# Mixture of experts: the second product of experts 1 to 7 with features on partitions, written at a register's column

## The chip, the cores and the metric

The kernel runs on one core of a Trainium2 chip. A core has TensorE (PE, with its weight loads PEld), VectorE (DVE), ScalarE (ACT), GpSimd (POOL) and SyncE (SP), each with an instruction queue of its own that is worked off in order, and 16 DMA engines. The metric is the device time of one execution in microseconds; three runs of the kernel before took 546.01, 545.29 and 543.28 us, median 545.29.

## What is computed

Three parts, one after the other. (1) A decayed linear attention over 2 x 8 heads gives x, 1536 tokens of 512 features. (2) A mixture of 8 experts with top-1 routing. (3) A dense layer, 512 to 2048 to 512 features, with a rational function between its products. The change lies in (2) and at its border to (3):

```python
gate_w = probs[np.arange(N), expert_idx]
for i in range(N):                       # first come, up to `capacity` a expert
    e = expert_idx[i]
    if counts[e] < capacity:
        disp[e, counts[e]] = x[i]; pos[i] = counts[e]; counts[e] += 1; keep[i] = True
h = np.maximum(np.einsum('ecd,edf->ecf', disp, w1), 0.0)      # 512 -> 1024
y = np.einsum('ecf,efd->ecd', h, w2)                          # 1024 -> 512
out[i] = gate_w[i] * y[expert_idx[i], pos[i]]                 # for kept i
```

The gate is a positive number for each token, and relu(g x) = g relu(x) for such a number, so the gate may be put on x or on y.

## The kernel before, in words

Every float product is done as three TensorE products of float32r parts: a value is split into a high part (ACT copies it, `whi`, `xh`, `hh`, `yh`) and the rest (DVE subtracts, `wlo`, `xl`, `hl`, `yl`), and high x high, high x low and low x high are summed in PSUM.

*Experts.* The program is written out by hand in the order in which each engine gets it. An expert has 224 slots, gathered from memory by token number as two tiles of rows (128 and 96; `gather`, POOL) and turned by PE so that features lie on partitions (`expert_x`: four 128x128 transposes, L822, then ACT writes `xh`, L825, and DVE `xl`, L826). Expert 0 goes through a special path (`first_expert`), experts 1 to 7 through the loop in `moe`. First product: four steps `fp`, each 24 matmuls (L852 to L854) with 128x128 weights standing and 224 columns of x moving; ACT takes the relu of a step (L857), DVE its rest (L858). In steps 2 and 3 the x rows of the next expert are turned. Second product: 48 matmuls (L885 to L887) with a slice of h standing (128 or 96 slots) and 512 weight columns moving, in four quarters of 12; so y comes out with slots on partitions. `y_out` scales it by the gate (ACT, L730), and POOL scatters the rows to memory tensor `yd` (L799), sorted by expert.

*Back again.* In experts 6 and 7 and in the first steps of the dense layer the 12 tiles of 128 sorted rows are loaded (`y_load`, SP, L959, tile `yr`) and turned by PE (`y_tile`, L972, PSUM tile `ytp`) into `yh` and `yl`, which the dense layer reads with features on partitions.

*Beside it.* In each of the eight slots of an expert `prep_next` asks SP for a half weight tile (512 KB into `raw`, six buffers) and splits the next one (ACT L136, DVE L142). `dec_slot` decodes the dense layer's weights, which come as 64 bit numbers, at every third slot from the third step of expert 1: two ACT scalings of the loaded tile (L186, L187) into `gq`, in the next slot two DVE bit operations (L194, L195) and a POOL addition (L198) into `dw`, later a store by SP to `wd` (L222). Tiles `gq` and the load's have two buffers each, and so has `dw`. Weights and decode loads and stores are all in SP's one queue.

*Overflow.* If an expert has more rows than slots, a branch at the end of expert 1 (`overflow`, L907 loads the flag into a register of every engine, L908 branches) redoes all experts in loops. With these inputs the branch is not taken.

Of the kernel before, what the change touches and what calls it, by code (L numbers as in the profile page):

```python
# [1 line left out]

# [28 lines left out]
W = 128 + W2  # L31
GROUPS = (0, 4, 7, 10, 12)
# [43 lines left out]
class Build:  # L76
# [15 lines left out]
    def setup(self):  # L92
# [25 lines left out]
        self.ovi = c.tile([1, 1], I32, name="ovi")  # L118
        self.xd = tc.dram_tile([NT, DM], F32, name="xd")
# [354 lines left out]
    def counts(self):  # L474
        nc = self.nc
        nc.vector.tensor_copy(self.off, self.cnt)
        nc.vector.tensor_tensor(out=self.off[:, 0:1], in0=self.off[:, 0:1], in1=self.pad, op=ALU.add)
        nc.vector.tensor_reduce(out=self.ovf, in_=self.off[0:1, 0:E], axis=AX.X, op=ALU.max)
        nc.vector.tensor_scalar(
            out=self.ovi, in0=self.ovf, scalar1=float(min(W, self.cap)), scalar2=None, op0=ALU.is_gt  # L480
        )
# [7 lines left out]
    def rows(self):  # L489
# [13 lines left out]
            op=ALU.add,  # L503
        )
# [219 lines left out]
    def win_out(self, acc, j):  # L724
        self.y_out(acc, 0, j)

    def y_out(self, acc, e, j):
        r = (128, W2)[j]
        y = self.mp.tile([128, 512], F32, tag="y", name="y", bufs=3)
        self.nc.scalar.activation(out=y[0:r], in_=acc[0:r], func=AF.Copy, scale=self.gate(e, j)[0:r])  # L730
        self.scatter(y[0:r], e, j)

    def first_expert(self):
# [8 lines left out]
        self.win_out(acc, 0)  # L742
# [22 lines left out]
        self.win_out(acc, 1)  # L765
# [28 lines left out]
    def scatter(self, t, e, j):  # L794
        s = self.slot(e, j)
        self.apart("yd", self.put_rows(t, self.sidx[0 : t.shape[0], s : s + 1]))

# [10 lines left out]
    def apart(self, key, i):  # L808
# [3 lines left out]
        self.puts[key].append(i)  # L812

# [16 lines left out]
    def moe(self):  # L830
        nc = self.nc
        with ExitStack() as st:
            self.dp = self.pool("dec", stack=st)
# [7 lines left out]
            for e in range(1, E):  # L841
                xh, xl = (t.pop(e)[:, :, 0:W] for t in (self.xh, self.xl))
                hh, hl = {}, {}
                for fp in range(4):
# [16 lines left out]
                    self.prep_next()  # L861
                    if fp >= 2 and e + 1 < E:
# [3 lines left out]
                    if e == E - 2 and fp >= 2:  # L866
                        for m in range(2):
                            self.y_load(2 * (fp - 2) + m)
# [6 lines left out]
                for hf in range(2):  # L875
                    i = 4 * e + 2 + hf
                    wh, wl = self.whi[i], self.wlo[i]
                    for m in range(2):
                        r = (128, W2)[m]
                        ms = slice(m * 128, m * 128 + r)  # L880
                        for fl in range(4):
                            f = hf * 4 + fl
                            fh, fo = hh[f // 2][:, f % 2, ms], hl[f // 2][:, f % 2, ms]
                            ws = slice(fl * 512, fl * 512 + 512)
# [3 lines left out]
                        if (e, hf, m) == (1, 1, 1):  # L888
                            self.overflow()
                        self.prep_next()  # L890
                        if e == E - 2:
                            self.y_tile(2 * hf + m, self.bank("tp", "ytp"))
                            self.y_load(4 + 2 * hf + m)
                        if 1 <= e < 5 and 2 * hf + m < 3:
                            self.perm_put(3 * (e - 1) + 2 * hf + m)
                        if e == 5 and hf == 1 and m == 1:
                            self.perm_get()
                        if hf == 1:
                            self.y_out(acc[m], e, m)
                        self.dec_slot(8 * e + 4 + 2 * hf + m)  # L900
                        if e == E - 1:
                            self.ffn_step(2 * hf + m)
                    del self.whi[i], self.wlo[i]

    def overflow(self):
        nc, tc = self.nc, self.tc
        v = nc.values_load(self.ovi[0:1, 0:1], min_val=0, max_val=1, skip_runtime_bounds_check_because="a flag")  # L907
        with tc.If(v > 0):  # L908
# [53 lines left out]
    def y_tile(self, t, tp):  # L962
# [8 lines left out]
        for k in range(4):  # L971
            nc.tensor.transpose(tp[:, k], y[:, k * 128 : k * 128 + 128], self.col("ident"))  # L972
# [310 lines left out]
```

## Time and profile before

| | before |
|---|---|
| median of 3 runs | 545.29 us (543.28 to 546.01) |
| the profiled execution | 545.39 us, of which the span of instructions is 543.6 |
| mean granted TensorE clock | 0.989 of full |
| PE, PEld, DVE, ACT, POOL busy | 96%, 81%, 76%, 72%, 52% |
| moved by DMA | 89.55 MB, 165 GB/s over the span |

Parts by the trace's time: attention and routing to about 84 us, expert 0 to 104, experts 1 to 7 to about 290 (the dense layer's first four steps are woven into expert 7), the dense layer to the end. The span is the time from the first to the last instruction. Busy shares count instructions that compute; a group's "waits" are the idle time of an engine just before an instruction, put down to what ended last.

### The profile page before, as it was taken

The numbers are of one execution on the slowest core, as the hardware profiler recorded it, in microseconds if no ns is written. First come the engines' busy times: TensorE is split into PE (matmuls) and PEld (weight loads), VectorE is DVE, ScalarE is ACT, GpSimd is POOL, SyncE is SP. The second block draws the span as 40 slices with busy tenths as digits, with TensorE's granted clock in tenths as the row PEclk, the third lists the DMA queues.
The fourth block names the chain that finished last, engine by engine and source line by source line (L and its number), as shares of the span: only waits on it lengthen the run. The fifth ranks groups of instructions, "written<-read, shape, count | busy, mean of one in ns | idle before, by whom it ended". The sixth has DMA issues, their size and how long they took to land.

```text
span 543.6 us, 9843 instructions
## 1 busy us (share of the span) xinstructions
PE 524.5 (96%) x3674; PEld 440.5 (81%) x3674; DVE 415.0 (76%) x630; ACT 391.4 (72%) x634; POOL 282.3 (52%) x212
## 2 busy tenths in 40 slices
PE   9999899999999999979999999999999999999993
PEld 4888777888898898959888888888888888888883
DVE  3548975768758797857667798999899998865972
ACT  2788952776567675836579798999999988676750
POOL 5554314307565675303144445675757765535664
PEclk9999999999999999979999999999999999999998
DMA  8998735695999999995505001230222200000203
GB/s 290 395 335 324 245 110 165 182 332 174 315 273 402 279 363 295 368 356 181 193 31 194 0 1 39 62 121 14 77 77 79 78 1 0 1 0 2 78 21 136
DMA packets 31044, 89.55 MB, mean 165 GB/s; under 512 B 6222, under 2 KB 6478, under 8 KB 30992
## 3 DMA queue, kind: packets, MB, share of 16 engines
q1 hardware_dynamic: 27216, 78.38, 42.7%
q0 software_dynamic: 3776, 10.50, 5.4%
q8 instruction: 30, 0.49, 0.4%
q14 instruction: 22, 0.18, 0.1%
HBM read 75.22 MB, written 14.16 MB: 164 GB/s over the span
## 4 chain that ended last, share of the span: by engine, by line
PE 53%; DMA 13%; issue 4%; DVE 2%; ACT 2%; POOL 1%; POOLq 0%; SPq 0%; ACTq 0%
DMA raw<-wm 9%; PE h L994 8%; PE h L992 8%; PE h L993 8%; PE o L1065 7%; PE o L1063 7%; PE o L1064 7%; DMA r<-wf 2%; DMA yr<-yd 1%; PE l L885 1%; PE l L886 1%; PE l L887 1%; PE ytp L972 1%; PE l L852 1%; ACT whi L136 1%
## 5 line engine op out<-in xcount | busy, mean ns | idle before, releaser
L142 DVE TENSOR_TENSOR wlo<-raw,whi 128x1024 fp32r<-128x1024 f32 x80 | 112.7, 1415 | 25.9 <-ACT whi L136 25.1
L1043 POOL TENSOR_TENSOR gg<-fx,gg 128x512 fp32r<-128x512 f32 x47 | 61.1, 1299 | 69.4 <-issue 60.6
L136 ACT ACTIVATE whi<-raw 128x1024 fp32r<-128x1024 f32 x80 | 84.2, 1056 | 16.3 <-DMA raw<-wm 15.9
L1063 PE MATMUL o<-whi,gg 128*128 128x512 f32 x192 | 74.9, 390 | 0.0
L992 PE MATMUL h<-yh,whi 128*128 128x512 f32 x192 | 74.8, 390 | 0.0
L994 PE MATMUL h<-yh,wlo 128*128 128x512 f32 x192 | 74.7, 389 | 0.0
L1065 PE MATMUL o<-whi,gg 128*128 128x512 f32 x192 | 74.7, 389 | 0.0
L1064 PE MATMUL o<-wlo,gg 128*128 128x512 f32 x192 | 74.7, 389 | 0.0
L993 PE MATMUL h<-yl,whi 128*128 128x512 f32 x192 | 74.7, 389 | 0.0
L1018 POOL TENSOR_TENSOR fw<-fh,fw 128x512 f32<-128x512 f32 x48 | 64.4, 1341 | 11.0 <-ACT fw L1007 11.0
L1005 ACT ACTIVATE fx<-h,ab 128x512 f32<-128x512 f32 x48 | 37.4, 779 | 38.4 <-PE h L994 38.2
L852 PE MATMUL l<-xh,whi 128*128 128x224 f32 x224 | 62.2, 278 | 0.3 <-PEq L908 0.3
L854 PE MATMUL l<-xh,wlo 128*128 128x224 f32 x224 | 61.5, 275 | 0.0
L853 PE MATMUL l<-xl,whi 128*128 128x224 f32 x224 | 61.4, 274 | 0.0
L198 POOL TENSOR_TENSOR dw<-gq 128x512 int32<-128x512 int32 x16 | 24.9, 1558 | 56.0 <-DVE gq L195 32.5
L885 PE MATMUL l<-whi,hh 128*128 128x512 f32 (+1 forms) x112 | 45.7, 408 | 0.0
L887 PE MATMUL l<-whi,hl 128*128 128x512 f32 (+1 forms) x112 | 44.8, 400 | 0.0
L886 PE MATMUL l<-wlo,hh 128*128 128x512 f32 (+1 forms) x112 | 44.7, 399 | 0.0
L852 PEld LDWEIGHTS l<-xh,whi 128*128 128x128 f32 x224 | 43.0, 192 | 1.1 <-issue 0.7
L853 PEld LDWEIGHTS l<-xl,whi 128*128 128x128 f32 x224 | 43.0, 192 | 0.2
L1029 DVE SCALAR_TENSOR_TENSOR fw<-fw,cq,h 128x512 f32<-128x512 f32 x48 | 35.6, 742 | 9.8 <-ACT h L1024 9.8
L854 PEld LDWEIGHTS l<-xh,wlo 128*128 128x128 f32 x224 | 43.0, 192 | 0.0
(161 smaller groups left out, 1267.9 us busy)
## 6 DMA issues: line engine op xcount, KB each, us to landing
raw<-wm SPq DMA_DIRECT2D x64, 512.0 KB, 9.7
r<-wf SPq DMA_DIRECT2D x32, 512.0 KB, 6.6
vq<-vq SPq DMA_DIRECT2D x11, 512.0 KB, 6.0
kk<-kk SPq DMA_DIRECT2D x11, 512.0 KB, 6.4
wd<-dw SPq DMA_DIRECT2D x16, 256.0 KB, 9.7
raw<-wd SPq DMA_DIRECT2D x8, 512.0 KB, 6.5
xd<-xs SPq DMA_DIRECT2D x12, 256.0 KB, 4.5
yr<-yd SPq DMA_DIRECT2D x12, 256.0 KB, 2.9
```

Source lines behind the costliest of these rows:

```text
L136: nc.scalar.activation(out=self.whi[i][:, sl], in_=raw, func=AF.Copy)
L142: nc.vector.tensor_tensor(out=self.wlo[i][:, sl], in0=raw, in1=self.whi[i][:, sl].bitcast(F32), op=ALU.subtract)
L852: nc.tensor.matmul(ps[:, fi], lhsT=wh[:, sl], rhs=xh[:, k], start=(k == 0), stop=False)
L853: nc.tensor.matmul(ps[:, fi], lhsT=wh[:, sl], rhs=xl[:, k], start=False, stop=False)
L854: nc.tensor.matmul(ps[:, fi], lhsT=wl[:, sl], rhs=xh[:, k], start=False, stop=(k == 3))
L992: nc.tensor.matmul(h, lhsT=wh[:, sl], rhs=yh[:, k], start=(k == 0), stop=False)
L993: nc.tensor.matmul(h, lhsT=wh[:, sl], rhs=yl[:, k], start=False, stop=False)
L994: nc.tensor.matmul(h, lhsT=wl[:, sl], rhs=yh[:, k], start=False, stop=(k == 3))
L1018: nc.gpsimd.tensor_tensor(out=w, in0=h2, in1=w, op=ALU.mult)
L1063: self.nc.tensor.matmul(ps, lhsT=gh[:, ms], rhs=wh[:, ws], start=first, stop=False)
L1064: self.nc.tensor.matmul(ps, lhsT=gh[:, ms], rhs=wl[:, ws], start=False, stop=False)
L1065: self.nc.tensor.matmul(ps, lhsT=gl[:, ms], rhs=wh[:, ws], start=False, stop=last)
```

## The change

In experts 1 to 7 the second product is turned round: 128x128 slices of the weights stand, and the 224 slots of h move, so y comes out with features on partitions. It is 96 matmuls an expert, into two PSUM tiles of two 224-column parts. ACT and DVE write it straight into `yh` and `yl`, now one tile each of 1536 + 224 columns, at the column where the expert's tokens start; that number is read into a register of ACT and of DVE (`start`). What an expert writes past its own tokens is written over by the next. The gate goes onto the gathered x rows, in place, on ACT (`x_gate`). Expert 0 keeps its form; its two y tiles are scaled as before and turned by PE (`y_turn`). Gone are the scatter of y to memory (but in the overflow body), the loads of it and their transposes. The decode adds in place into the first half of `gq` and has no tile of its own. The overflow body takes its tiles from the buffers of hh and hl.

```diff
@@ class Build
     def dec_spill(self, n):
-        w = self.dp.tile([128, 512], I32, tag="dw", name="dw", bufs=2)
-        self.dec_dve(n, w)
-        self.w32[n] = w.bitcast(F32)
+        g = self.gq[n][0][:, 0]
+        self.dec_dve(n, g)
+        self.w32[n] = g.bitcast(F32)
...
-    def win_out(self, acc, j):
-        self.y_out(acc, 0, j)
-
-    def y_out(self, acc, e, j):
+    def y_rows(self, acc, j):
         r = (128, W2)[j]
-        y = self.mp.tile([128, 512], F32, tag="y", name="y", bufs=3)
-        self.nc.scalar.activation(out=y[0:r], in_=acc[0:r], func=AF.Copy, scale=self.gate(e, j)[0:r])
-        self.scatter(y[0:r], e, j)
+        y = self.wp.tile([128, 2, 512], F32, tag="wt", name="y", bufs=3)[0:r, 0]
+        self.nc.scalar.activation(out=y, in_=acc[0:r], func=AF.Copy, scale=self.gate(0, j)[0:r])
+        return y
+
+    def y_turn(self, y, j):
+        r = y.shape[0]
+        tp = self.bank("tp", "ytp").rearrange("p (k n) -> p k n", k=4)[:, :, 0:r]
+        for k in range(4):
+            self.nc.tensor.transpose(tp[:, k], y[:, k * 128 : k * 128 + 128], self.col("ident")[0:r, 0:r])
+        self.y_put(tp, slice(0, 4), bass.ds(self.start(0), r) if j else slice(0, r))
+
+    def y_put(self, ps, k, at):
+        yh, yl = self.yh[:, k, at], self.yl[:, k, at]
+        self.nc.scalar.activation(out=yh, in_=ps, func=AF.Copy)
+        self.nc.vector.tensor_tensor(out=yl, in0=ps, in1=yh.bitcast(F32), op=ALU.subtract)
+
+    def start(self, e):
+        lo, hi = (max(0, NT - (E - e) * W), NT) if e else (0, 128)
+        return self.nc.values_load(
+            self.st8[0:1, e : e + 1],
+            engines=(mybir.EngineType.Activation, mybir.EngineType.DVE),
...
@@ def first_expert(self):
-        self.win_out(acc, 0)
+        y = self.y_rows(acc, 0)
...
         self.win_l1(x, ps, 12, 18)
+        self.y_turn(y, 0)
         ht0 = self.win_split(h, 0, bank("l1"))
         self.win_l1(x, ps, 18, 24)
         self.win_relu(ps, h, 1)
+        self.x_gate(1, 0)
+        self.x_gate(1, 1)
         self.expert_x(1, 0)
...
-        self.win_out(acc, 1)
+        self.y0 = self.y_rows(acc, 1)
...
+    def x_gate(self, e, j):
+        x = self.xg[2 * e + j]
+        self.nc.scalar.activation(out=x, in_=x, func=AF.Copy, scale=self.gate(e, j))
...
@@ def moe(self):
                     self.prep_next()
+                    if 1 <= fp < 3 and e + 1 < E:
+                        self.x_gate(e + 1, fp - 1)
                     if fp >= 2 and e + 1 < E:
                         self.expert_x(e + 1, fp - 2)
...
                     self.dec_slot(8 * e + fp)
-                    if e == E - 1:
-                        self.y_tile(4 + fp, self.bank("tp", "ytp"))
-                        if fp >= 2:
-                            self.y_load(6 + fp)
-                acc = [self.bank("l2") for _ in range(2)]
...
-                            nc.tensor.matmul(acc[m][0:r], lhsT=fh, rhs=wh[:, ws], start=(f == 0), stop=False)
-                            nc.tensor.matmul(acc[m][0:r], lhsT=fh, rhs=wl[:, ws], start=False, stop=False)
-                            nc.tensor.matmul(acc[m][0:r], lhsT=fo, rhs=wh[:, ws], start=False, stop=(f == 7))
...
+                    if (e, fp) == (1, 0):
+                        self.y_turn(self.y0, 1)
+                acc = [self.bank("l2").rearrange("p (a n) -> p a n", a=2)[:, :, 0:W] for _ in range(2)]
+                for q in range(4):
+                    wh, wl = self.whi[4 * e + 2 + q // 2], self.wlo[4 * e + 2 + q // 2]
+                    for f in range(2 * q, 2 * q + 2):
+                        fh, fo = hh[f // 2][:, f % 2], hl[f // 2][:, f % 2]
+                        for o in range(4):
+                            ws = slice(f % 4 * 512 + o * 128, f % 4 * 512 + o * 128 + 128)
+                            mm = partial(nc.tensor.matmul, acc[o // 2][:, o % 2], skip_group_check=True)
+                            mm(lhsT=wh[:, ws], rhs=fh, start=(f == 0 and o % 2 == 0), stop=False)
+                            mm(lhsT=wh[:, ws], rhs=fo, start=False, stop=False)
+                            mm(lhsT=wl[:, ws], rhs=fh, start=False, stop=(f == 7 and o % 2 == 1))
+                    if (e, q) == (1, 3):
+                        self.overflow()
+                    self.prep_next()
...
+                    if q == 3:
+                        at = bass.ds(self.start(e), W)
+                        for i in range(2):
+                            self.y_put(acc[i], slice(2 * i, 2 * i + 2), at)
+                    self.dec_slot(8 * e + 4 + q)
+                    if e == E - 1:
+                        self.ffn_step(q)
...
@@ def build(arrays, capacity):
-    nc = bacc.Bacc("TRN2", target_bir_lowering=False, num_devices=1)
+    nc = bacc.Bacc("TRN2", target_bir_lowering=False, num_devices=1, dynamic_dma_scratch_size=8192)
```

## Rows read from the trace of the kernel before

**Rows 1.** The page, part 1: busy us, share of the span, instructions.
```profile
PE 524.5 (96%) x3674; PEld 440.5 (81%) x3674; DVE 415.0 (76%) x630; ACT 391.4 (72%) x634; POOL 282.3 (52%) x212
```
**Rows 2.** Waits of PE: what, for whom, us in total, times, longest.
```profile
PE ytp L972 <- DMA yr<-yd: 3.9, 1, 3.9
```
**Rows 3.** Windows: length, busy PE, PEld, DVE, ACT, POOL, clock, DMA share, GB/s.
```profile
150.00:172.00 22.00, 22.00 (x149) 19.39 (x149) 15.33 (x18) 14.42 (x22) 12.01 (x9) 1.00 0.98 320
...
231.00:236.00 5.00, 1.07 (x6) 0.64 (x5) 3.34 (x3) 0.49 (x1) 0.66 (x1) 0.87 1.03 397
236.00:242.00 6.00, 6.00 (x20) 4.22 (x18) 1.92 (x2) 2.67 (x4) 0.00 (x0) 0.54 1.02 398
```
**Rows 4.** Timeline of ACT, experts 2 and 3: start, us, operation, idle before.
```profile
141.66 0.66 ACT L186 ACTIVATE gq<-r 128x512 f32<-128x512 f32 x1 [1.56 <-DMA r<-wf]
...
150.30 0.69 ACT L186 ACTIVATE gq<-r 128x512 f32<-128x512 f32 x1
...
155.89 1.06 ACT L136 ACTIVATE whi<-raw 128x1024 fp32r<-128x1024 f32 x1 [0.30 <-DMA raw<-wm]
161.36 0.66 ACT L186 ACTIVATE gq<-r 128x512 f32<-128x512 f32 x1 [4.41 <-DMA r<-wf]
```
**Rows 5.** Timeline of PE around the first y tile, expert 6.
```profile
231.41 0.39 PE L887 MATMUL l<-whi,hl 128*128 128x512 f32 x1
235.73 1.09 PE L972 MATMUL ytp<-ct,yr 128*128 128x128 f32 x4 [3.93 <-DMA yr<-yd]
...
241.67 0.60 PE L972 MATMUL ytp<-ct,yr 128*128 128x128 f32 x4
```
**Rows 6.** Groups of PE by form: count, busy us, mean ns, idle before.
```profile
L972 PE MATMUL ytp<-ct,yr 128*128 128x128 f32 x48 | 7.4, 285 | 3.9 <-DMA yr<-yd 3.9
```
**Rows 7.** Timeline of PE, expert 3: the two turns of x rows.
```profile
157.53 0.60 PE L822 MATMUL tp<-ct,xg 128*128 128x128 f32 x4
...
160.65 0.60 PE L822 MATMUL tp<-ct,xg 128*128 128x128 f32 x4
```
**Rows 8.** Timeline of PE, experts 4 and 5: second product, then first.
```profile
189.20 0.39 PE L885 MATMUL l<-whi,hh 128*128 128x512 f32 x1
...
194.70 0.26 PE L852 MATMUL l<-xh,whi 128*128 128x224 f32 x1
...
202.74 0.60 PE L822 MATMUL tp<-ct,xg 128*128 128x128 f32 x4
```
**Rows 9.** Timeline of PE, expert 0: the turn of expert 1's first x rows.
```profile
96.99 0.60 PE L822 MATMUL tp<-ct,xg 128*128 128x128 f32 x4
```
**Rows 10.** Timeline of ACT in the same stretch.
```profile
97.18 0.59 ACT L697 ACTIVATE h<-l 96x512 f32<-96x512 f32 x1 [0.89 <-PE l L688]
97.68 0.58 ACT L825 ACTIVATE xh<-tp 128x512 fp32r<-128x512 f32 x1
```
**Rows 11.** Timeline of SP: issues of the stores of decodes 1, 2 and 3.
```profile
135.54 0.38 SPq L222 DMA_DIRECT2D wd<-dw  x1
...
139.32 0.53 SPq L222 DMA_DIRECT2D wd<-dw  x1
...
148.73 0.33 SPq L222 DMA_DIRECT2D wd<-dw  x1
```
**Rows 12.** Line 222 in the windows of these three issues: time to landing.
```profile
DMA to landing us min/median/max: 9.6/9.6/9.6
...
DMA to landing us min/median/max: 13.3/13.3/13.3
...
DMA to landing us min/median/max: 15.6/15.6/15.6
```
**Rows 13.** Line 907: ACT's load of the flag, ns.
```profile
L907 ACTq TENSOR_LOAD <-ovi x1: 460/460/460, 123.8 to 123.8; - x1
```
**Rows 14.** Waits of SP: its branch.
```profile
SPq L908 <- SPq L908: 7.6, 1, 7.6
```

More of the change, by code (lines that the diff above doesn't have):

```diff
@@ L1 @@
 from contextlib import ExitStack
+from functools import partial
 import concourse.bass as bass
@@ L503, in rows @@
             op=ALU.add,
+        )
+        nc.vector.scalar_tensor_tensor(
+            out=self.st8, in0=self.ov.to_broadcast([1, E]), scalar=float(NT), in1=off[0:1], op0=ALU.mult, op1=ALU.max
+        )
+        nc.vector.tensor_scalar(
+            out=self.st8[:, 0:1], in0=self.pad[0:1], scalar1=-1.0, scalar2=128.0, op0=ALU.mult, op1=ALU.add
         )
@@ L722, in win_l2 @@
             )
-    def win_out(self, acc, j):
-        self.y_out(acc, 0, j)
-    def y_out(self, acc, e, j):
+    def y_rows(self, acc, j):
         r = (128, W2)[j]
-        y = self.mp.tile([128, 512], F32, tag="y", name="y", bufs=3)
-        self.nc.scalar.activation(out=y[0:r], in_=acc[0:r], func=AF.Copy, scale=self.gate(e, j)[0:r])
-        self.scatter(y[0:r], e, j)
+        y = self.wp.tile([128, 2, 512], F32, tag="wt", name="y", bufs=3)[0:r, 0]
[16 more added lines that the diff above has]
+            engines=(mybir.EngineType.Activation, mybir.EngineType.DVE),
+            min_val=lo,
+            max_val=hi,
+            skip_runtime_bounds_check_because="no expert before it exceeds its slots, or all go behind the last row",
+        )
     def first_expert(self):
@@ L927, in overflow @@
                 for fh in range(2):
-                    w = self.yp.tile([128, 4, 512], F32, tag="yl1", name="ow", bufs=1)
-                    nc.sync.dma_start(out=w.rearrange("p k n -> p (k n)"), in_=wm[fh])
+                    w = [tmp(f"hl{k}") for k in range(4)]
+                    for k in range(4):
+                        nc.sync.dma_start(out=w[k], in_=wm[fh][:, k * 512 : k * 512 + 512])
                     for f in range(4 * fh, 4 * fh + 4):
@@ L940, in overflow @@
                             )
[L941 removed]
+                        nc.scalar.activation(out=hs[fh][:, fs], in_=ps, func=AF.Relu)
                 py = self.bank("l1", "opy")
                 for fh in range(2):
[L944 to L945 removed]
+                    w = [tmp(f"hl{k}") for k in range(4)]
+                    for k in range(4):
+                        nc.sync.dma_start(out=w[k], in_=wm[2 + fh][:, k * 512 : k * 512 + 512])
                     for f in range(4 * fh, 4 * fh + 4):
@@ L955, in overflow @@
                 self.put_rows(xg, gi[:, 1:2])
-    def y_load(self, t):
-        y = self.xp.tile([128, DM], F32, tag="xg", name="yr", bufs=4)
-        self.nc.sync.dma_start(out=y, in_=self.yd[t * 128 : t * 128 + 128, :])
-        self.yr[t] = y
-    def y_tile(self, t, tp):
-        nc = self.nc
-        tb, r = divmod(t, 4)
-        if r == 0:
-            p = self.yp if tb < 2 else self.fp
-            self.yh[tb] = p.tile([128, 4, 512], F32R, name=f"yh{tb}")
-            self.yl[tb] = p.tile([128, 4, 512], F32R, name=f"yl{tb}")
-        y = self.yr.pop(t)
-        tp = tp.rearrange("p (k n) -> p k n", k=4)
-        for k in range(4):
-            nc.tensor.transpose(tp[:, k], y[:, k * 128 : k * 128 + 128], self.col("ident"))
-        sl = slice(r * 128, r * 128 + 128)
-        nc.scalar.activation(out=self.yh[tb][:, :, sl], in_=tp, func=AF.Copy)
-        nc.vector.tensor_tensor(
-            out=self.yl[tb][:, :, sl], in0=tp, in1=self.yh[tb][:, :, sl].bitcast(F32), op=ALU.subtract
-        )
+            with tc.For_i(0, NTILE, 1) as t:
+                y = tmp("hh0")
+                rows = self.yd.rearrange("(t p) n -> t p n", p=128)[bass.ds(t, 1)]
+                nc.sync.dma_start(out=y, in_=rows.rearrange("one p n -> (one p) n"))
+                tp = self.bank("tp", "otp").rearrange("p (k n) -> p k n", k=4)
+                for k in range(4):
+                    nc.tensor.transpose(tp[:, k], y[:, k * 128 : k * 128 + 128], self.col("ident"))
+                self.y_put(tp, slice(0, 4), bass.ds(t * 128, 128))
     def ffn_at(self, n):
@@ L1106, in ffn @@
             self.fp = self.pool("ffn", stack=st)
-            for t in range(10, NTILE):
-                self.y_load(t)
             for n in range(4, NA):
@@ L1130, in ffn_step @@
         self.ffn_do("g")
-        for t in {4: (8, 9), 5: (10, 11)}.get(n, ()):
-            self.y_tile(t, self.bank("tp" if n == 4 else "l2", "ytp"))
         if not soon:
@@ L1144, in ffn_step @@
             self.ffn_p(n - 1)
-        self.ffn_b([(n - lb, m) for m in range(2 if n == lb else 4)])
+        self.ffn_b([(n - lb, m) for m in range(4)])
         self.put_outs()
```

78 lines of the change are left out of this document (26 added, 52 removed).

## The prediction

> **What bounds the kernel now.** I read the page's engine row first: PE is busy for 96% of the span and beside its own weight loads (81%) nothing passes 76% [rows 1]. Then the waits of PE: one item stands out, the transposes of the y rows that come back from memory, 3.9 us in one wait [rows 2]. The windows say what the clock did there: 0.87 granted in the stretch with the wait, 0.54 in the 6 us behind it, and 1.00 in the expert stretch shown [rows 3]; 2.4 GHz is full, 1.2 GHz half. So before the wait PE runs without a hole; what shortens the time is fewer TensorE microseconds, or that hole. The DMA column has a second reading: share 0.98 in expert 3 and 1.02 to 1.03 around the hole. The transfers are the resource that is nearly full, and ACT (ScalarE), in order, waits for them: 4.41 us before one gq decode [rows 4]. PE does not feel that today, since only relu results, split x and weights come to it from ACT, and the last relu of an expert is first read three quarters into an 11 us product.
>
> The sum is made against the profiled execution's 545.39 us (span 543.6), which is 0.1 us from the median of the three runs, 545.29.
>
> **What is removed.**
> 1. *The hole.* The last matmul before it starts at 231.41 and would be followed 0.23 later; the transposes start at 235.73: 4.1 us. From 235.73 to 241.67, 5.94 us, PE does one tile's transposes and 12 matmuls at half clock [rows 5]. At full clock that is 0.44 + 12 x 0.229 = 3.19 (both worked out below), so 2.75 more. The yr<-yd load that ended the wait no longer exists. Together 6.85.
> 2. *Transposes.* 48 of them in 12 tiles [rows 6]. In expert 3 two tiles' starts, 157.53 and 160.65, are 3.12 apart with 24 matmuls of 0.1117 between (2.68), so four transposes with the restart cost 0.44 [rows 7]. 12 x 0.44 = 5.3.
> 3. *Second product.* Before: 24 matmuls of 512 columns from 189.20 to 194.70, 0.229 each, 48 an expert: 11.0. After: 96 of 224 columns with 128-column weights, which is the form of the first product: 72 of them from 194.70 to 202.74, 0.1117 each, 10.7 [rows 8]. Saved 0.3 x 7 experts = 2.1.
> A rule of the Trainium skill (page TensorE: Matmul & The Clock Gate, section Back-to-back issue gap) would give more: it has N/2.4 + 2.5 ns for N columns, 215.8 and 95.8 ns, hence 1.16 us an expert, 8.1 in all, and the sum would be 536.0. This trace differs: 111.7 ns at 224 columns. The Trainium skill, same page, section LDWEIGHTS (loading the stationary operand), gives 106.7 ns for 128 weight columns, near the 111.7, so it fits to read the narrow matmul as bound by its weights.
> 4. *Scatters and y loads* (16 and 12 DMAs): POOL and queue time. I take it as nothing on PE directly; it thins the full DMA stage (used in 7).
> Removed: 6.85 + 5.3 + 2.1 = 14.25.
>
> **What is added.**
> 5. *Two turns* of expert 0's rows, four transposes each: 0.8. Their y rows leave ACT well before PE asks (2.7 us of matmuls lie between in the second case).
> 6. *Gate on x, expert 0.* Both x_gate stand on ACT behind the relu of h, and PE's next instruction is the transpose of the gated rows. Today that transpose starts at 96.99, relu runs 97.18 to 97.77 and ACT's next starts at 97.68. The gate, 128x512 like the 0.66 us gq scaling, would end near 98.35 and PE start at 98.45: 1.45 of hole [rows 4, 9, 10]. Nothing covers it. The bounds are 1.2 (ACT overlaps) and 2.1 (PE waits for both).
> 7. *Gate and decode, experts 2 and 3.* Two edits act together. x_gate puts PE's transposes behind ACT's queue, with about 0.5 us in hand: relu, split (1.05) and gate (0.66) against 2.7 us of matmuls. And the decode now adds in place into gq, so the decode's first ACT instruction must wait until the store of two decodes earlier has landed. Today only POOL waited for that. Behind it on ACT stand relus, splits, gates and evictions, and PE waits for the gates. Landings: the stores issued at 135.54, 139.32 and 148.73 took 9.6, 13.3 and 15.6, so they land at 145.1, 152.6 and 164.3, while the decodes that would wait for them start at 141.66, 150.30 and 161.36 [rows 4, 11, 12]: 3.4, 2.3 and 2.9 late. I take 0.5 us off the first two and 1.9 off the third for the missing scatters (estimate: the third lies 14 us into the full DMA stretch, and four scatters of some 0.5 us of DMA time have dropped out by then). Followed on, in today's times: decode 4 runs 152.1 to 153.35; then split, register load (0.46, [rows 13]), two evictions, two relus and two splits bring the first gate of expert 3's turn to 159.25, where PE, 0.6 earlier by item 3, is ready at 156.9: 2.4. PE reaches the second gate at 162.5. Decode 5 waits to 162.4, ends 163.65, then relu, split and gate: 165.65, 3.2 late. Sum 5.6; in expert 2 I count 0.3. From then on PE is some 5 us later than today while the transfers are not, and the same walk finds ACT level with PE through experts 4 to 6. Bounds: 0 (the transfers catch up) and, by the unchanged 161.36 plus every store wait handed on, 9.
> 8. *The clock.* Holes of 2.4 and 3.2 us, 2.7 apart. The trace shows the fall after 4.1 [rows 3, 5]; 3.2 is nearer to that than to none, so I take the same 2.75. Bounds 0 and 5.5 (both holes, or also item 6).
> 9. *Register loads*, eight on ACT and eight on DVE: 0.46 each on queues with idle time; their share stands in 7. *Evictions*: ACT has two of 448 columns for two of 512, 12 eviction pairs of y tiles leave ACT and DVE, 14 pairs arrive; PE needs the bank only a product (11 us) later. Expert 7's eviction stands ahead of the fourth step of the last stage; if that step waited for it, three passes of 0.59 (two on ACT, one more on DVE), 1.8 at most. I take 0, since it reads columns 0 to 511, which expert 7 can't reach.
> Added: 0.8 + 1.45 + 5.9 + 2.75 = 10.9.
>
> Sum: 545.4 - 14.25 + 10.9 = **542.0**. Own range 538 to 546.
>
> **Rivals.**
> - *ACT is on time* (chance 0.18). The missing scatters shorten the queue enough; 7 is 0.3 and 8 is 0: 545.4 - 14.25 + 2.55 = 533.7. For: DMA share 0.98 is only just full. Against: ACT waits 4.41 us in expert 3 even without the new wait.
> - *Narrow matmuls run at column rate* (0.03): 224/512 of 0.229 is 0.100, 96 of them 9.6, saving 9.7 in place of 2.1: 534.4. Against: the first product has this very form at 0.1117. The Trainium skill (TensorE: Matmul & The Clock Gate, Back-to-back issue gap) has the spacing follow the columns, as this rival does.
> - *The branch holds ACT* (0.12). The overflow body now uses the hh and hl tiles, and SP takes 7.6 us over its branch, waiting for transfers [rows 14]. If expert 2's first relu waits for SP, it is some 4 us late and the gate hands that to PE: 546, no change. For: tiles shared with a skipped body. Against: PE, which reads banks that the body writes, goes straight on today.
> - *The store loop sets the pace* (0.17): slower. From a decode's start to the issue of its store pass 148.73 - 141.66 = 7.1; with a landing of 13.3 that is 20.4 for two decodes, while two decodes have 6 of the 8 slots of an expert, 6/8 of 10.7 + 10.7 + 0.9 = 16.7. Each of the six pairs would then lose 3.7, 22 in all, through the gates: 545.4 - 14.25 + 2.25 + 22 = 555. It decides from a landing of 16.7 - 7.1 = 9.6 upward; against it, an ACT that waits stops asking for weights, and the queue before the store empties.
>
> **How the numbers follow.** My forecast has 0.50. About 0.5%, 2.7 us, is what a measurement can tell from no change, so faster means below 542.7 and slower above 548.1. Of the forecast I put 0.28 below, 0.21 between and 0.01 above; the first two rivals are faster (0.21), the branch is mostly no change (0.10, 0.02 slower), the store loop slower (0.17, 0.01 of it no change if the landings are short). Rounded: faster 0.49, same 0.31, slower 0.20. The range takes in the first two rivals and the shorter landings of the last: 532 to 552.
>
> **What would show it.** No ytp wait and no half clock after expert 6; 0.112 between starts of the second product's matmuls; one hole of about 1.5 us before expert 1's first x transposes, ended by ACT's gate; two holes ended by the gate in expert 3's turn, a fall of the clock behind them; the gq scaling waiting for the store's DMA by 2 to 3 us. The forecast is wrong if PE shows no holes in experts 2 to 6 (533.7), if they recur in each (555), or if the second product's spacing is not 0.112.

## The result, and the profile after

The changed kernel takes 538.14 us (median of 4 runs, 537.23 to 539.89) against 545.65 for the kernel before beside it (4 runs, 543.28 to 547.05): a ratio of 0.987, 95% interval 0.983 to 0.991. In a second comparison on another chip it took 537.77 (6 runs, 536.3 to 540.48) against 546.1 (10 runs, 543.65 to 550.42): 0.984, 0.980 to 0.989. One run of the kernel before on that chip, and one of a variant below, were over 1.5% longer at a lower clock and are left out. So on these two chips the change is worth 7.5 and 8.3 us. That is not a property of the kernels alone: on two other chips the kernel before itself ran in 536.68 (one run) and 540.98 us (median of 7), and a variant of the changed kernel that differs by a shift of its constants took 536.47 on the first of them.

The forecast was 542.0, own range 538 to 546: sign and range held, the sum did not. Two steps of it (items 7 and 8, 8.65 us) did not happen, and two costs of together 5 us that it had not foreseen took much of their place. That 538.14 still lies in the range, by 0.14 us, is luck.

The profiled execution took 538.44 us, span 536.7. Page, part 1, of the kernel after (answers to [rows 1]; columns as there):

```profile
PE 518.7 (97%) x3970; PEld 450.7 (84%) x3970; DVE 418.9 (78%) x637; ACT 392.6 (73%) x638; POOL 260.9 (49%) x196
```

Waits of PE after (answers to [rows 2]). The first row is the attention part's and has a like one before (3.2). The wait for the y rows is gone; two new ones stand in the list, at the branch (L937) and at expert 0's gate (L844):

```profile
PE sc L288 <- issue: 3.5, 4, 1.4
PE l L883 <- PEq L937: 1.6, 1, 1.6
PE tp L854 <- ACT xg L844: 1.3, 1, 1.3
```

Windows after, same bounds as [rows 3]: no hole and no half clock in expert 6.

```profile
150.00:172.00 22.00, 21.98 (x197) 21.80 (x197) 18.82 (x22) 17.29 (x25) 11.64 (x9) 1.00 0.98 314
231.00:236.00 5.00, 5.00 (x47) 5.00 (x46) 4.96 (x8) 4.13 (x8) 1.30 (x1) 1.00 0.91 278
236.00:242.00 6.00, 6.00 (x56) 6.00 (x56) 5.97 (x6) 3.26 (x5) 2.05 (x1) 1.00 0.98 363
```

Second product, PE timeline after, expert 4 (answers to [rows 8]): 95 spacings from the second matmul to the first of expert 5 are 10.61 us, 0.1117 each, as forecast.

```profile
186.87 0.27 PE L911 MATMUL l<-hl,whi 128*128 128x224 f32 x1
...
197.48 0.27 PE L883 MATMUL l<-xh,whi 128*128 128x224 f32 x1
```

Where the 6.9 us of span went, from the starts of the same matmuls in both timelines (the forecast column sorts its items by place):

| stretch | before | after | moved | forecast |
|---|---|---|---|---|
| up to expert 1 | 103.74 | 105.81 | +2.07 | +1.85 |
| expert 1 | 23.06 | 24.45 | +1.39 | +0.1 |
| experts 2 to 5 | 90.52 | 89.52 | -1.00 | +7.45 |
| expert 6 | 31.11 | 22.31 | -8.80 | -8.9 |
| expert 7 to dense step 8 | 55.30 | 52.48 | -2.82 | -3.8 |
| dense steps 8 to 47 | 212.16 | 215.55 | +3.39 | 0 |
| step 47 to the end | 27.71 | 26.58 | -1.13 | 0 |

Three stretches are off: the experts that were to lose 7.45 and won 1.0, the branch at the end of expert 1, and a dense layer that the change hardly touches and that became 3.4 us slower. The last 1.13 lie behind the last matmul, in a closing instruction of POOL, the longest (the last figure before the comma, in ns) of three of one kind: before, after, and in the changed kernel with a scatter put back behind each of experts 1 to 7 (below).

```profile
L1270 POOLq DRAIN  x3: 45/113/6573, 536.2 to 543.3; - x3
```
```profile
L1281 POOLq DRAIN  x3: 40/113/5369, 530.5 to 536.4; - x3
```
```profile
L1286 POOLq DRAIN  x3: 45/113/6438, 531.4 to 538.4; - x3
```

So the missing scatters save about 1.1 us at the end. Of the 0.98 by which the stretch from expert 7 to dense step 8 falls short, 0.33 is the length of the rows of `yh` and `yl` (52.16 with longer ones, below) and 0.28 a new wait of PE for DVE at 277.9 us; the rest was not followed up.

### The profile page after: what moved, and what is told of

Its sections match the earlier page's. It is cut to its first block, busy times and chain, and to the rows that moved or that the text cites. A ratio compares the mean times of both kernels' runs of the same rounds, so it can differ in the third digit from the quotient of the medians.

```text
span 536.7 us, 10429 instructions
## 1 busy us (share of the span) xinstructions
PE 518.7 (97%) x3970; PEld 450.7 (84%) x3970; DVE 418.9 (78%) x637; ACT 392.6 (73%) x638; POOL 260.9 (49%) x196
## 4 chain that ended last, share of the span: by engine, by line
PE 70%; issue 2%; POOL 1%; ACT 1%; DVE 1%; POOLq 0%; ACTq 0%
PE h L1009 8%; PE h L1010 8%; PE h L1011 8%; PE o L1080 7%; PE o L1082 7%; PE o L1081 7%; PE l L883 4%; PE l L885 4%; PE l L884 4%; PE l L911 4%; PE l L912 4%; PE l L910 4%; POOL out L1111 1%; PE tp L854 1%; ACT fh L1040 0%
## 5 line engine op out<-in xcount | busy, mean ns | idle before, releaser
L1080 PE MATMUL o<-whi,gg 128*128 128x512 f32 x192 | 75.7, 394 | 0.0
L1082 PE MATMUL o<-whi,gg 128*128 128x512 f32 x192 | 75.5, 393 | 0.0
L202 POOL TENSOR_TENSOR gq<-gq 128x512 int32<-128x512 int32 x16 | 25.0, 1561 | 84.6 <-DVE gq L199 60.7
L910 PE MATMUL l<-hh,whi 128*128 128x224 f32 x224 | 61.9, 276 | 0.0
L911 PE MATMUL l<-hl,whi 128*128 128x224 f32 x224 | 61.5, 274 | 0.0
L912 PE MATMUL l<-hh,wlo 128*128 128x224 f32 x224 | 61.4, 274 | 0.0
L1082 PEld LDWEIGHTS o<-whi,gg 128*128 128x128 f32 x192 | 36.0, 187 | 8.5
L1009 PEld LDWEIGHTS h<-yh,whi 128*128 128x128 f32 x192 | 36.0, 188 | 8.5 <-DVE fx L1048 0.7
```

What stands on the lines that cost most here:

```text
L910: mm(lhsT=wh[:, ws], rhs=fh, start=(f == 0 and o % 2 == 0), stop=False)
L1009: nc.tensor.matmul(h, lhsT=wh[:, sl], rhs=self.yh[:, k, ts], start=(k == 0), stop=False)
L1080: self.nc.tensor.matmul(ps, lhsT=gh[:, ms], rhs=wh[:, ws], start=first, stop=False)
L1082: self.nc.tensor.matmul(ps, lhsT=gl[:, ms], rhs=wh[:, ws], start=False, stop=last)
```

## Experiments

The theory after this result: PE bounds the kernel throughout; expert 0's gate and the branch each open a hole; ACT's wait for the decode's stores is real, but PE, made late by these holes, does not meet it. Against it stood the forecast's own reason for "ACT is on time": the missing scatters relieve the transfers.

### The dense layer: addresses or row length

In the changed kernel 512-column matmuls are 224 to 238 ns apart where before all were 226 to 227. The change added two small constants (36 bytes a partition) ahead of every later tile, and made the rows of `yh` and `yl` 7040 bytes long (2048 before). Four edits tell the two apart: constants shifted back, longer rows, constants shifted in the kernel before, and 1024 unused bytes behind unchanged rows.

```diff
-        c.tile([128, 24], F32, name="align")
+        c.tile([128, 15], F32, name="align")
```

> The changed kernel with the unused filler tile among the constants cut from 24 to 15 floats a partition, so that all tiles behind the two new small constants (9 floats) lie at the addresses of the kernel before. Nothing is computed differently. Theory A (addresses): the dense layer's 512-column matmuls, 227 to 238 ns apart in the changed kernel and 226.7 before, were slowed by the 36 bytes; they return to 227, dense steps 8 to 47 take 212.2 us in place of 215.5, and the time falls by 3.4 us to about 534.8. Rival B (row stride): it is the new 7040-byte rows of yh and yl (2048 before) that slow them; spacing stays at 230 and the time at 538.1. Rival C (clock or chip): the spacing changes from run to run; no pattern by line.

```diff
-            self.yh, self.yl = (yp.tile([128, 4, NP], F32R, name=n) for n in ("yh", "yl"))
+            self.yh, self.yl = (yp.tile([128, 4, 1792], F32R, name=n) for n in ("yh", "yl"))
```

> The changed kernel with yh and yl 1792 columns long in place of 1760, so that a row of them is 7168 bytes, a multiple of 1024; the constants stay as they are. Theory A (addresses moved by the 36 bytes of the constants): dense spacing stays at 227 to 238 ns, time 538.1. Rival B (row stride): spacing returns to 227 ns, dense steps 8 to 47 take 212.2 us, time about 534.8.

In the kernel before:

```diff
-        c.tile([128, 24], F32, name="align")
+        c.tile([128, 33], F32, name="align")
```

> The kernel before with the filler tile grown from 24 to 33 floats, so that what lies behind it moves by the same 36 bytes as in the changed kernel; nothing else. Theory A (addresses): its 512-column matmuls go from 226.7 to 230 ns apart, steps 8 to 47 of the dense layer from 212.2 to about 215.6 us, the second product of the experts (also 512 columns) too, and the time rises by 3 to 4 us. Rival B (row stride): no change, 545.3.

And, in the changed kernel, with a second edit that is read at the branch (below):

```diff
             self.yh, self.yl = (yp.tile([128, 4, NP], F32R, name=n) for n in ("yh", "yl"))
+            yp.tile([128, 256], F32, name="hole")
...
                 nc.scalar.activation(out=xg, in_=py, func=AF.Copy, scale=ga)
                 self.put_rows(xg, gi[:, 1:2])
-            with tc.For_i(0, NTILE, 1) as t:
-                ...
-                self.y_put(tp, slice(0, 4), bass.ds(t * 128, 128))
```

> The changed kernel with two edits that are read at two places. (1) An unused tile of 1024 bytes a partition behind yh and yl: what lies behind them moves as it did with the longer rows, but the rows keep 7040 bytes. If the row length makes the dense layer's 512-column matmuls slow, steps 8 to 47 stay at 215.5 us; if it was where the tiles behind them lie, they take 212.2. (2) The skipped overflow body without its last loop, which rebuilds the y operand (left out; these inputs don't run it). If the length of the skipped body makes PE's branch slow, its 2.9 us and the 1.6 us of idle PE shrink; if the branch costs the same 3 us before and after, and only the matmuls queued ahead of it, narrow now, cover less of it, both stay. Time 538 with both rivals' no.

One window of 200 us inside the dense layer shows it in the number of matmuls that PE starts (the first bracket). Before, after, shifted constants, longer rows, and the 1024 bytes behind unchanged rows, in this order:

```profile
300.00:500.00 200.00, 200.00 (x884) 165.61 (x883) 177.30 (x249) 173.08 (x271) 119.89 (x90) 1.00 0.12 37
```
```profile
300.00:500.00 200.00, 200.00 (x871) 162.93 (x870) 174.44 (x245) 171.34 (x269) 119.26 (x89) 1.00 0.12 37
```
```profile
300.00:500.00 200.00, 200.00 (x870) 162.99 (x869) 174.41 (x245) 169.77 (x266) 120.65 (x90) 1.00 0.11 37
```
```profile
300.00:500.00 200.00, 200.00 (x884) 165.59 (x883) 176.75 (x249) 172.78 (x271) 122.06 (x91) 1.00 0.11 37
```
```profile
300.00:500.00 200.00, 200.00 (x870) 162.97 (x869) 174.45 (x244) 170.55 (x267) 120.59 (x90) 1.00 0.11 38
```

All show PE 100% busy at clock 1.00; the share says nothing, the count does: 884 against 870. The first matmuls of dense steps 8 and 47, after and with the longer rows:

```profile
294.57 0.39 PE L1009 MATMUL h<-yh,whi 128*128 128x512 f32 x1
...
510.12 0.39 PE L1009 MATMUL h<-yh,whi 128*128 128x512 f32 x1
```
```profile
294.59 0.39 PE L1009 MATMUL h<-yh,whi 128*128 128x512 f32 x1
...
506.75 0.39 PE L1009 MATMUL h<-yh,whi 128*128 128x512 f32 x1
```

Steps 8 to 47 take 215.54 us with shifted constants, 212.16 with rows of 7168 bytes, 215.54 with the 1024 bytes behind, and 212.16 in the kernel before with its constants shifted. So the addresses theory falls, and so does the place of the tiles behind: the row length is the cause, or the start of `yl`, which moves with it (not told apart). Single runs: 536.47 for the shifted constants and 535.08 for the longer rows on one chip, 537.16 for the 1024 bytes on another.

### The hole of the kernel before varies

On the chip of the first three of these runs the kernel before ran once in 536.68 us, and its shifted copy took 540.69. PE timelines at the first y transposes, of the shifted copy and of a second profile of the unchanged kernel before (answers to [rows 5]):

```profile
233.71 0.63 PE L972 MATMUL ytp<-ct,yr 128*128 128x128 f32 x4 [2.01 <-DMA yr<-yd]
```
```profile
235.65 1.09 PE L972 MATMUL ytp<-ct,yr 128*128 128x128 f32 x4 [5.07 <-DMA yr<-yd]
```

Windows behind them, in the same order: the clock stays full behind 2.0 us of hole and falls behind 5.1, as it did behind 3.9 [rows 3, 5].

```profile
236.00:242.00 6.00, 6.00 (x32) 4.72 (x31) 4.61 (x6) 3.82 (x7) 1.80 (x1) 1.00 1.00 376
```
```profile
235.00:242.00 7.00, 6.35 (x27) 4.94 (x28) 2.49 (x3) 3.87 (x6) 0.00 (x0) 0.76 1.04 400
```

> The kernel before as it is, for a second profile on this chip. Theory H: the time from the last 12 matmuls ahead of the first y transposes to expert 7 shows a wait for the y rows of 0 to 4 us, and the time above 536.5 is this wait, plus 2.75 us where the clock falls behind it. Rival: experts and dense layer differ too, by a few us all along (a slower chip).

> The changed kernel as it is, against the kernel before on the same chip, five times. A single run of the kernel before on the chip of the first experiments took 536.7 us, against 543.3 to 547.1 in the earlier runs, and the shifted one there had a wait of 2.0 us for the y rows with the clock full behind it, against 3.9 us and half clock. Theory H (the hole varies): the kernel before is 536.5 us plus the hole for the y load plus the half clock behind it, and its time spreads from 536 to 547 with the chip's transfers; the changed kernel has no such wait and stays at 536 to 540. Where the hole is small, the change is worth 0 to -1 us; where it is 4 us with the clock's fall, 7.5. Rival: the low single run was a chance, and the ratio stays at 0.987.

Measured: 543.88 for the profiled run before, 537.77 (536.3 to 540.48) for the changed kernel. Expert 6 takes 26.47, 30.81 and 31.11 us in the three profiles of before, 24.38 by its parts (22.62 and four tiles at 0.44); so the hole, with the half clock behind it, is 2.1, 6.4 and 6.7 us. To leave the attention part out, whose length differs by up to 4 us between profiles, take the time from one matmul of expert 0 to the end. In the first profiles of before and after it is this one:

```profile
88.29 0.47 PE L716 MATMUL l<-whi,ht 128*128 128x512 f32 x1
```
```profile
88.39 0.48 PE L726 MATMUL l<-whi,ht 128*128 128x512 f32 x1
```

From there to the end the kernel before takes 450.8, 455.2 and 455.3 us, less the hole 448.7, 448.7 and 448.6. The changed kernel takes 448.3, and 450.3 in a second profile, where the clock fell behind the branch (below). So the change is worth the hole of the run that it is compared with and little else; its other savings were spent. This is shown for these profiles, and only argued for the low times of the kernel before, whose traces are not at hand (536.68 here, 537.21 to 544.03 on one more chip). The rival holds for the two chips on which both were timed several times: there the ratio stays near 0.985.

### Expert 0's gate

```diff
         ht0 = self.win_split(h, 0, bank("l1"))
+        self.x_gate(1, 0)
+        self.x_gate(1, 1)
         self.win_l1(x, ps, 18, 24)
         self.win_relu(ps, h, 1)
-        self.x_gate(1, 0)
-        self.x_gate(1, 1)
```

> The changed kernel with the two gate scalings of expert 1's x rows on ACT placed ahead of the second relu of expert 0, in front of the last 6 matmuls of its first product, in place of behind that relu. Theory: the 1.5 us hole before expert 1's first x transposes is ACT's two gates and the relu in one row; with the gates done earlier the hole falls to 0.2 and every later landmark moves 1.2 to 1.5 us ahead, time about 536.7. Rival: PE waits there for the relu anyway, or the time given back at expert 0 is lost again in experts 2 and 3, where PE would come earlier than the transfers and ACT; then holes ended by ACT's gate appear there and the time stays at 538.

PE timeline, changed kernel and this one:

```profile
99.01 0.66 PE L854 MATMUL tp<-ct,xg 128*128 128x128 f32 x4 [1.29 <-ACT xg L844]
```
```profile
97.10 0.66 PE L854 MATMUL tp<-ct,xg 128*128 128x128 f32 x4
```

The two scalings no longer stand between PE's matmuls and the transposes: the hole is gone, the transposes start 1.05 us behind the first matmul of the group ahead of them instead of 2.38, and no hole opens in experts 2 and 3. The single time, 536.35, has the attention part's spread in it (expert 1 starts at 103.9 to 106.2 in these runs).

### The branch

```diff
-                    if (e, q) == (1, 3):
-                        self.overflow()
```

> The changed kernel without the branch at the end of expert 1 and the body behind it (left out: the redo for experts with more rows than slots, which these inputs don't need). Theory: the 1.6 us that PE stands there is the 2.9 us that its sequencer takes over the branch, less the matmuls that it has queued ahead; without it expert 2 starts 1.6 us earlier and the time falls by as much, to about 536.5. Rival: PE waits there for relu or split as well, or what it gains is lost in experts 2 and 3, where PE would come earlier than ACT and the transfers; then holes ended by ACT's gate appear there, and the time stays.

Expert 1 shrinks from 24.45 to 22.66 us: PE's wait at L937 is gone. What was gained there is lost in expert 3, which takes 24.39 us in place of 22.54. PE and ACT timelines without the branch, expert 3:

```profile
163.10 0.66 PE L854 MATMUL tp<-ct,xg 128*128 128x128 f32 x4 [1.61 <-ACT xg L844]
```
```profile
151.70 0.67 ACT L190 ACTIVATE gq<-r 128x512 f32<-128x512 f32 x1 [5.99 <-DMA wd<-gq]
...
159.81 0.68 ACT L190 ACTIVATE gq<-r 128x512 f32<-128x512 f32 x1 [1.71 <-DMA wd<-gq]
160.39 0.67 ACT L191 ACTIVATE gq<-r 128x512 int32<-128x512 uint32 x1
160.97 0.52 ACT L888 ACTIVATE hh<-l 128x448 fp32r<-128x448 f32 x1
161.40 1.04 ACT L140 ACTIVATE whi<-raw 128x1024 fp32r<-128x1024 f32 x1
162.34 0.70 ACT L844 ACTIVATE xg<-xg,tab 128x512 f32<-128x512 f32 x1
```

This is the chain that item 7 described: the decode's first ACT instruction waits for the landing of an earlier store, and behind it on ACT stand relu, split and the gate that PE needs. It is the second half of the rival's sentence, and the time, 537.59, shows no gain; from the matmul of expert 0 to the end it is 448.2 us, against 448.3 with the branch.

The branch's own rows, kernel before, changed kernel, and the one without the body's last loop (ns, then the start in us):

```profile
L908 PEldq COMPARE_BRANCH  x1: 353/353/353, 122.8 to 122.8; - x1
```
```profile
L937 PEldq COMPARE_BRANCH  x1: 2865/2865/2865, 127.1 to 127.1; - x1
```
```profile
L937 PEldq COMPARE_BRANCH  x1: 2685/2685/2685, 125.9 to 125.9; - x1
```

A shorter body leaves the branch and its 1.45 us of idle PE as they are, so the loop at its end, all that the new body adds to PE's matmuls, is not what makes it slow. The expectation's other reading, that the branch costs 3 us in both kernels and only its cover shrank, does not fit: before, the branch itself reads 0.35 and is over 3.3 us before the product's last matmul ends. (PE stands 0.30 us idle there before too.) Why TensorE's sequencer needs 2.7 to 3.2 us there in each of the eight profiles with it is open. The Trainium skill, Advanced Engine Details and Errata, Control Flow Timing, has 108 ns for a compare-and-branch; ACT's is recorded with 50 here, PE's with 353 before and 2865 after, and the measurement decides.

### Is it the scatters?

```diff
                             self.y_put(acc[i], slice(2 * i, 2 * i + 2), at)
+                        for j in range(2):
+                            s, r = self.slot(e, j), (128, W2)[j]
+                            self.apart("yd", self.put_rows(zz[0:r], self.sidx[0:r, s : s + 1]))
```

> The changed kernel with a scatter to memory put back behind each of experts 1 to 7: two indirect transfers of 128 and 96 rows from a tile of zeros into the memory tensor that nothing reads in this kernel; no wait of PE or ACT hangs on them. Theory R (relief): the changed kernel shows no holes in experts 2 to 6 because the scatters are gone and what ACT waits for lands earlier; with them back, weight landings go from 9.0 to about 11 us, ACT's store wait grows, and PE shows holes of 1 to 3 us ended by ACT's gate in expert 3, time 539 to 542. Rival S (slack): the missing holes come from PE's own delay of 1.3 us at the gate and 1.6 at the branch, which ACT and the transfers use; then the scatters change nothing, PE shows no new holes, 538.

Time to landing of the weight loads (`raw`) issued from 126 to 175 us, in the kernel before, the changed kernel, and with the scatters back:

```profile
DMA to landing us min/median/max: 4.3/12.0/16.2
```
```profile
DMA to landing us min/median/max: 5.4/9.0/11.0
```
```profile
DMA to landing us min/median/max: 4.7/8.8/11.7
```

And of the decode's stores (`wd`) issued in the same stretch, changed kernel and with the scatters back:

```profile
DMA to landing us min/median/max: 6.2/8.5/10.8
```
```profile
DMA to landing us min/median/max: 6.1/7.7/12.4
```

The software queue's share rose from 3.8% to 5.2%, so the scatters were there. The weight loads land no later, against theory R. The stores do in part: those of decodes 1 and 2 take 10.3 and 12.4 us against 8.7 and 10.8, that of decode 3 takes 7.7 against 9.6, and ACT's longest wait for one is 5.20 against 3.75 (1.65 in the second profile of the changed kernel), as theory R had it:

```profile
154.79 0.66 ACT L190 ACTIVATE gq<-r 128x512 f32<-128x512 f32 x1 [5.20 <-DMA wd<-gq]
```

PE shows no new hole, as theory S had it, and the time, 540.41, lies in theory R's range for other reasons. But this run is a weak test of both, since PE came late to expert 3: it lost 2.2 us at the branch and then the clock. The second profile of the changed kernel did the same; from the matmul of expert 0 to the end it takes 450.3 us and this run 451.3, and the 1.0 between them is POOL's closing instruction. PE timeline and windows of that second profile:

```profile
130.87 0.34 PE L883 MATMUL l<-xh,whi 128*128 128x224 f32 x1 [2.22 <-PEq L937]
```
```profile
130.80:133.00 2.20, 2.13 (x14) 2.16 (x15) 0.38 (x1) 0.00 (x0) 0.43 (x1) 0.73 0.06 6
133.00:136.00 3.00, 3.00 (x19) 3.00 (x19) 0.00 (x0) 0.56 (x2) 0.00 (x0) 0.63 0.17 16
```

The granted clock falls behind these 2.2 us (to a mean of 0.63 over 3 us), where it stayed at 1.00 behind 1.6; expert 2's first product took 13.2 us there, 11.57 in the first profile. Whether the dropped scatters help to keep PE without holes is not settled by this run.

### All together, and the decode's own tile

Longer rows and early gates in one kernel, all else as changed:

> The changed kernel with yh and yl rows of 7168 bytes and the two gates of expert 1's x rows ahead of expert 0's second relu: both edits that paid alone. Theory: they add up, -3.4 us in the dense layer (spacing 226.7 ns) and -1.3 to -1.5 at expert 0, so 4.8 us below the changed kernel, about 533.3, and below the kernel before even in its best runs. Rival: earlier by 1.5 us, PE meets ACT's store wait in experts 2 and 3, and only the 3.4 are left.

Measured: 532.45 (5 runs, 532.24 to 534.47) against 537.77 for the changed kernel on the same chip, 5.3 less, and 0.975 (0.971 to 0.980) of the kernel before. Without the attention part, from the matmul of expert 0 to the end, the profiles have 443.4 and 448.3 us: 4.9 less, where the longer rows alone gave 3.7 and the early gates alone 1.5. So the edits add up to within 0.4 us; in expert 3 PE meets a wait of 0.26 us for the gate. This version is faster than the kernel before even without its hole (448.6).

Then the same without the branch:

> The changed kernel with 7168-byte rows, the early gates, and no branch (left out: the redo for experts with more rows than slots). So PE loses neither the 1.3 us at expert 0 nor the 1.6 us at expert 1's end. Theory S: what PE gains there it loses in expert 3, where ACT, after its waits for the decode's stores, is late with the gate: without the branch alone the second hole was 1.6 us; now PE comes 1.4 us earlier still and the holes in experts 2 and 3 sum to about 3 us, perhaps with the clock's fall behind them; time 532.5 to 535, no better than with the branch (532.9). Rival: ACT moves ahead with PE, the holes stay at 1.6, and the time is 531.3 or less.

And with it the decode's sum in a tile of its own:

```diff
-        g = self.gq[n][0][:, 0]
-        self.dec_dve(n, g)
-        self.w32[n] = g.bitcast(F32)
+        w = self.dw[:, n % 2]
+        self.dec_dve(n, w)
+        self.w32[n] = w.bitcast(F32)
```

> The kernel with 7168-byte rows, early gates and no branch, and the decode's sum written into a tile of its own (two halves of a spare buffer) in place of gq's first half, so that the wait for the store is POOL's and not ACT's (left out, as there: the redo of overflowing experts). Theory: the holes of expert 3 come from the in-place decode, so ACT's store wait (6 us before the first of its decodes in expert 3) goes, ACT has the gate ready in time, the holes of 1.6 to 3 us vanish, and the time is 530 to 531.5. Rival: ACT waits as long for the decode's load or the weights as it waited for the store; the holes and the time stay.

Windows of the two, 150 to 172 us; then PE's holes in the first of them:

```profile
150.00:172.00 22.00, 20.37 (x181) 20.00 (x180) 19.29 (x23) 17.49 (x26) 10.67 (x8) 1.00 0.98 330
```
```profile
150.00:172.00 22.00, 22.00 (x200) 22.00 (x199) 18.16 (x23) 15.22 (x22) 10.69 (x9) 1.00 1.01 304
```
```profile
156.85 0.66 PE L854 MATMUL tp<-ct,xg 128*128 128x128 f32 x4 [1.21 <-ACT xg L844]
160.60 0.66 PE L854 MATMUL tp<-ct,xg 128*128 128x128 f32 x4 [0.42 <-ACT xg L844]
```

With the in-place sum PE loses 1.63 us at the two gates; with its own tile nothing. Expert 3's first product takes 13.57 and 11.51 us, and from expert 1's start to the end 427.0 and 425.0 pass. Medians: 531.16 (4 runs, 530.96 to 531.62) and 530.65 (5 runs, 529.85 to 533.5). These ranges overlap: the medians alone do not show the gain, and expert 1 starts 4.2 us later in the second profile. So the in-place decode costs 2.06 us once PE is on time: shown, by taking away only what makes ACT wait. The first expectation was wrong in its size: PE came 1.4 us earlier still and lost no more than before, so ACT moved ahead with it, as the rival had it.

## Why the prediction was right, and where it was wrong

*Items 1 to 3* held. Expert 6 is shorter by 8.80 us against 8.9 forecast (hole and half clock 6.85, four tiles, product); the product's 0.3 an expert measured 0.29 to 0.33. The hole's size is that of the profiled run, not of the kernel: 2.1 to 6.7 us in three profiles.

*Item 4*, the relief by the missing scatters, was put to nothing on PE, and at the end of the kernel it is 1.1 us. Its use in 7 (2.9 us off the landings) is borne out in part: with the scatters back the stores of decodes 1 and 2 take 1.6 us longer, but that of decode 3, off which the walk took 1.9, takes 1.9 less. Weight loads land earlier than before (9.0 us against 12.0), with the scatters back too (8.8); in the kernel with neither the late gate nor the branch it is 10.7, so a part comes from PE's stops there. The rest is open.

*Items 5 and 6*: turns and gate, 1.85 forecast by expert 1, 2.07 measured, of which 0.1 is the attention part's; the hole is 1.29, ended by ACT's gate, as said.

*Item 7* is the step that failed: 5.9 us of holes forecast, 0.2 measured (expert 3 takes 22.54 us, the ones behind it 22.31). The mechanism is there (the decode waits for the store, and the gate behind it on ACT is late); the walk's times for PE and for one store were wrong. ACT timeline after (answers to [rows 4]):

```profile
152.16 0.66 ACT L190 ACTIVATE gq<-r 128x512 f32<-128x512 f32 x1 [3.75 <-DMA wd<-gq]
...
159.58 0.71 ACT L844 ACTIVATE xg<-xg,tab 128x512 f32<-128x512 f32 x1
160.66 0.69 ACT L190 ACTIVATE gq<-r 128x512 f32<-128x512 f32 x1 [0.37 <-DMA wd<-gq]
...
163.20 0.70 ACT L844 ACTIVATE xg<-xg,tab 128x512 f32<-128x512 f32 x1
```

Decode 4 waits and starts at 152.16; the forecast said 152.1. Decode 5 starts at 160.66 against 162.4, for its store, issued at 150.95, took 9.6 us and not the 13.7 that the walk gave it. The first gate starts at 159.58 (the forecast had it done at 159.25), the second at 163.20 (it had it done at 165.65). And PE, said to be ready at 156.9 and 162.5, asks at 160.67 and at about 163.7: it is 3.1 us later than before. The walk moved PE forward by item 3's 0.6 and forgot the sum's own items 5 and 6, 2.25 us, which lie ahead of it; the branch added the rest. Worked out with the 2.25, the first of the two holes (2.4) would have been 0.1. The second (3.2) would have stayed: it went because decode 5 started 1.7 us sooner, so that the gate was done at 163.9, and because PE came 1.2 later. What the mechanism costs without PE's delay, the last two runs show: 2.06 us.

*Item 8* went with it: holes of 1.6, 1.3, 1.2 and 0.4 left the clock at 1.00. Where it fell, behind 2.2 us at the branch in two profiles, no term had a place for it; expert 2 takes 1.6 us longer there.

*Item 9* held for the register loads and the evictions: no wait of PE ends on them. It named no cost for two things that the change carried along: the branch (1.4 to 2.2 us of PE, 0.3 before) and the row length (3.4 in steps 8 to 47).

*The rivals.* "ACT is on time" gave PE without holes in experts 2 to 6, and that is what came, but not by the transfers alone: without the branch the holes are there, with the scatters gone all the same, so it took PE's own delay. And it came without its 533.7. "The branch holds ACT" had the right place and the wrong engine: PE stood there, and the argument against it, that PE goes straight on, was read from the branch of before, which is short (0.35). Narrow matmuls at column rate and the store loop did not come: 0.1117 us and no recurring holes. That the weight loads set this pace, as item 3 reads it, no run tests.

The sum again: 542.0, less 8.65 for items 7 and 8, plus 1.6 and 3.4, is 538.35; the profiled run took 538.4. That it fits so well is luck in part: the 1.0 us short in expert 7 and the 1.1 us saved at the end are left out, and cancel.

## What to carry to other kernels

A walk of one engine against another has to carry every delay that one's own sum puts ahead of it; a wait that is real may lie hidden behind another cost and come out when that is mended, so mend both and look again. When a layout changes, count the matmuls in a window of a stage that only reads the new tile: a busy share of 100% at full clock hid 1.6%. And a time that contains one long wait for a transfer is the time of one run: get a second profile before pricing its removal. To compare two kernels by their profiles, count from a matmul that both have, behind the part that varies.

## What the runs showed of the hardware

- The row length of a moving operand's tile (or the start of the second tile, which moves with it) set the pace of 512-column matmuls: 7040 bytes gave 5526 ns for each dense step of 24, 7168 and 2048 bytes 5440, to within 1 ns in all 39 steps. The slow pattern begins at the fourth matmul of a step, the first that reads the tile's second row, and goes on through matmuls that do not read it. Why is open.
- One untaken branch held TensorE's sequencer for 2.7 to 3.2 us in eight profiles of the changed kernel and its variants, and 0.35 in three of before.
- A hole of 2.2 us was followed by a stretch at half clock in two profiles (the granted clock is 0.61 to 0.76 on the mean of 2 to 3 us there); one of 2.0 us in the shifted kernel before, and one of 1.9 at the branch, were not.
- POOL's closing DRAIN took 6.57 us in the kernel before and 5.37 without its 16 scatters; with 14 of them put back it took 6.44.
